# One adaLN training step on one core: w_mod's gradient blocks earlier, three kinds of stores on other queues, two transposed loads ahead of the last phase

## The chip, the cores and the metric

The kernel runs on 1 core of a Trainium2 chip. A core has a matrix engine (TensorE, PE in the profile; its weight loads are PEld), VectorE (DVE), ScalarE (ACT), GpSimd (POOL) and SyncE (SP), which here issues DMAs only. DMAs can be issued from SP's, ACT's and POOL's queues. Each engine and each queue works through its instructions in a fixed order; an instruction that waits holds up everything behind it.

The metric is device time in microseconds (us) of one execution. Before the change the median of 8 runs is 433.16 us (431.62 to 435.19).

## The reference, cut to what matters

A block of an adaptive-LayerNorm network, its output and the gradients of nine of its inputs. S = 2048 rows, D = 512 columns, F = 1792 hidden columns, all in bf16.

```
mod = silu(c) @ w_mod                        # six rows of D: sa, ca, ga, sb, cb, gb
h = layernorm(x) * (1 + ca) + sa
x = x + ga * irfft2(rfft2(h) * (w_r + 1j * w_i))
h = layernorm(x) * (1 + cb) + sb
x = x + gb * (relu(h @ w1 + b1) ** 2 @ w2 + b2)
# jax.vjp of this with grad_out:
# returns x and the gradients of x, w_r, w_i, w1, b1, w2, b2, c, w_mod
```

The kernel's outputs are numbered 0 (x), 1 (gradient of x), 2 and 3 (w_r, w_i), 4 (w1), 5 (b1), 6 (w2), 7 (b2), 8 (c) and 9 (w_mod, 512 x 3072, computed in six column blocks of 512).

## The kernel before, in words

Rows sit on the 128 partitions, 16 rows each, so that x is a tile of 128 x 16 x 512 and a "row tile" t holds 128 rows. Fourier transforms are products with small cosine and sine matrices. The kernel has four stretches in time:

1. 0 to about 93 us: layernorm, the forward spectral filter, and the product of grad_out with w2 (`back_products`, line 700).
2. 93 to 282 us: the dense part in four blocks of 512 rows (`stage_h`, `stage_o`, `stage_gn`). It leaves in DRAM what the end needs: `h_dram` (the hidden activations), `n1_dram` (normalised rows) and `gx1_dram` (a part of x's gradient).
3. 282 to about 352 us, the way back through the filter (lines 1049 to 1204). `spec_f23` (line 299) runs over eight groups gi. For each, PE makes psB and psC, ACT copies them (AE, then G, line 313), and DVE does the complex products of `ew_b` (line 1140, `cmul` line 414): first Z times G, which `spec_g1` will need, then X times G, the gradient gW of the filter, which goes out in four stores per group (line 1146; six for group 0). After each group `after_b` (line 1148) loads a later group and calls `fill_w1`, which puts one or two of 16 units of w1's gradient on PE (`grad_w1`, line 1100: 16 products of 128 x 448, one copy by ACT at line 1108, and after each second unit one store at line 1110). After groups 1, 3, 5 and 7 it calls `GMod.emit` (line 452), a block of w_mod's gradient, here "gm block". Then `spec_g1` (line 336) multiplies the eight Z by LG; its 16 results are copied out of PSUM by DVE (line 351) and ACT (line 353) in turn, four PSUM buffers at a time.
4. 352 us to the end. Eight row pairs (`row_pair`, line 1240, t = 0, 2, ... 14) finish x's gradient; each is a chain of ACT copies of psY (line 1249), DVE work (lines 250 to 270 and 1251 to 1265), two ACT sums (line 1253) and a store of gx (line 1266). A row pair reads `n1` at line 1254 and `gxl` at line 1265; `load_rows3` (line 1190) loads them two row pairs ahead into two buffers each, so a load has to wait until the row pair before last has read its buffer. Between row pairs 14 units of w2's gradient run (`grad_w2`, line 1170): 16 products of 128 x 512 with `hn` and `g_sb`, a DVE product into gw (line 1176, three buffers), a store (line 1177). `hn` is a transposing load from `h_dram` (line 1168), 512 KB each; `g_sb` is grad_out, 2 MB, one load at line 1196. Two more gm blocks and c's gradient end the kernel.

A gm block broadcasts one gradient row over the partitions with PE (line 457), copies it with ACT (gmbc, one buffer, line 459), scales it by silu(c) into gwm (two halves by ACT, two by DVE, lines 467 and 469) and stores gwm (line 472); and it multiplies four 128 x 512 pieces of w_mod (wmc, loaded at line 463) with gmbc on DVE and sums them (gm_junk, line 470).

The order of the work is set when the program is built: the code is written in a rough order with priorities, a list scheduler orders each engine and queue, and semaphores are put in. Tiles come from pools with a number of buffers (`bufs`). Pools are stacked from the left and from the right end of the on-chip memory, so a new pool may lie where an old one was, and its first user then waits for the old one's last readers, stores among them. PSUM for the units (`mm`) has two buffers.

Nearly all DMAs of stretches 3 and 4 are issued by SP, stores included. POOL issues only the loads of w_r and w_i in stretch 1 (line 548), ACT three small loads at the start.

Of the kernel before, what the change touches and what calls it, by code (L numbers as in the profile page):

```python
# [12 lines left out]
BF16 = mybir.dt.bfloat16  # L13
# [430 lines left out]
class GMod:  # L444
# [3 lines left out]
    def __init__(self, tc, K, scf, gsc, wm_view, out9_view):  # L448
        self.__dict__.update(locals())
        self.bufs = 2  # L450

    def emit(self, jc, q, row, pool, ppool):

        nc, K = self.tc.nc, self.K
        cs = slice(jc * D, (jc + 1) * D)
        psb = ppool.tile([P, D], FP32, name="mm")
        nc.tensor.matmul(psb, lhsT=K["ones_sq"][q:q + 1, :], rhs=row, start=True, stop=True, tile_position=(q, 0))
        gmbc = pool.tile([P, D], BF16, name="gmbc", bufs=1)
        nc.scalar.copy(out=gmbc, in_=psb)
        junk = pool.tile([P, D], BF16, name="gm_junk", bufs=1)  # L460
        for dc in range(0, 4, 2):
            wmc = pool.tile([P, 2, D], BF16, name="wmc", bufs=self.bufs)
            nc.sync.dma_start(wmc, self.wm_view[:, dc:dc + 2, cs])
            gwm = pool.tile([P, 2, D], BF16, name="gwm", bufs=self.bufs)
            for i in range(2):
                if i == 0:
                    nc.scalar.activation(gwm[:, i, :], gmbc, AF.Copy, scale=self.scf[:, dc + i:dc + i + 1])
                else:
                    nc.vector.tensor_scalar(gwm[:, i, :], gmbc, self.scf[:, dc + i:dc + i + 1], None, op0=ALU.mult)
                nc.vector.scalar_tensor_tensor(out=junk, in0=wmc[:, i, :], scalar=K["onef"], in1=gmbc, op0=ALU.mult, op1=ALU.mult,  # L470
                                               accum_out=self.gsc[:, jc, dc + i:dc + i + 1])
            nc.sync.dma_start(self.out9_view[:, dc:dc + 2, cs], gwm)


@with_exitstack
def kernel(
# [571 lines left out]

    gm = GMod(tc, K, scf, gsc, wm_view, out9_view)
    lf2 = tc.alloc_tile_pool(name="lf2", bufs=1, side="right")  # L1050
    K["LF"] += [lf2.tile([P, 2, 3, P], BF16, name=f"LFb{gi}") for gi in range(4, 8)]
    W4 = 448
# [47 lines left out]
    def grad_w1(fb, dc):  # L1100
        fs = slice(fb * W4, (fb + 1) * W4)
        ps = mmps.tile([P, SB], FP32, name="mm")
        for t in range(NT):
            nc.tensor.matmul(ps[:, 0:W4], lhsT=h2_sb[:, t, dc * P:(dc + 1) * P], rhs=ghn[t // 4][:, t % 4, fs],  # L1104
                             start=(t == 0), stop=(t == NT - 1))
        if fb % 2 == 0:
            w1o[0] = gwa.tile([P, 2, W4], BF16, name="gw1", bufs=2)
        nc.scalar.copy(out=w1o[0][:, fb % 2, :], in_=ps[:, 0:W4])  # L1108
        if fb % 2 == 1:
            nc.sync.dma_start(out4_view[:, dc, (fb - 1) * W4:(fb + 1) * W4], w1o[0].rearrange("p a f -> p (a f)"))  # L1110

# [7 lines left out]
    def fill_w1(n):  # L1119
        for _ in range(n):  # L1120
            if units:
                units.pop(0)()

    gms = [lambda j=j, q=q, row=row: gm.emit(j, q, row, gwa, mmps)
           for j, q, row in ((5, 0, grow[0:1, :]), (2, 32, grow[32:33, :]), (3, 64, grow[64:65, :]), (4, 0, gcrow))]

    with tc.tile_pool(name="f23b", bufs=2) as fr, tc.tile_pool(name="ewb", bufs=2) as ew:
# [9 lines left out]
        for gi in range(4):  # L1137
            load(gi)

        def ew_b(gi, G):  # L1140
# [3 lines left out]
            for i, o in enumerate((out_2, out_3)):  # L1144
                for p0_, n, rows_ in w_parts(o, gi):
                    nc.sync.dma_start(rows_, gW[p0_:p0_ + n, i, :, 0:DF])

        def after_b(gi):
# [4 lines left out]
            fill_w1(2 if 0 < gi < 6 else 1)  # L1153
            if gi % 2 == 1:
                gms.pop(0)()

        spec_f23(tc, K, UT, AEs, None, lambda gi: gwa.tile([P, 2, 2, FP], BF16, name="G", bufs=2), ew_b, after_b)
    lf2.release()
    gwp = tc.alloc_tile_pool(name="gwp", bufs=1, side="right")
    g_sb = gwp.tile([P, NT, D], BF16, name="g_sb")  # L1160

    hns, endp = [], {}

    def load_hn():
        fc = len(hns)
        if fc < NFC:
            hns.append(endp.get("hn", gwp).tile([P, NT, P], BF16, name="hn", bufs=4))
            nc.sync.dma_start(hns[fc], h_dram[fc, :, :], transpose=True)

    def grad_w2(fc):  # L1170
# [4 lines left out]
        with tc.high_priority():  # L1175
            nc.vector.tensor_tensor(gw, ps, modb[:, GB_B, :], op=ALU.mult)  # L1176
        nc.sync.dma_start(out6_view[:, fc, :], gw)
        load_hn()
# [16 lines left out]

    nc.sync.dma_start(g_sb, g_view)
    load_hn()
    load_rows3(0)
    load_rows3(2)
    for _ in range(3):  # L1200
        load_hn()
# [9 lines left out]
    def fill(n):  # L1211
        for _ in range(n):
            if units:
                fill_w1(1)
                if not units:
                    gwa.release()
                    gap.release()
                    gm.bufs = 4
                    endp["hn"] = endp["gm"] = tc.alloc_tile_pool(name="endp", bufs=2)
# [8 lines left out]
    with tc.tile_pool(name="psE", bufs=2, space=PSUM) as psE, tc.tile_pool(name="psS1", bufs=1, space=PSUM) as psS1:  # L1228
# [11 lines left out]
        def row_pair(t, Ts):  # L1240
# [65 lines left out]
    fin.release()  # L1306
    gwp.release()
    h2p.release()
    cdp.release()
# [36 lines left out]
```

## Time and profile before

| what | value |
|---|---|
| time of the profiled execution | 433.14 us |
| its span (first to last instruction) | 431.4 us |
| median of 8 runs | 433.16 us (431.62 to 435.19) |
| PE busy | 400.2 us, 93% |
| DVE busy | 353.6 us, 82% |
| ACT busy | 256.4 us, 59% |
| POOL busy | 41.1 us, 10%, nothing after slice 6 |
| DMA | 101.11 MB, 234 GB/s on average |
| mean granted clock of TensorE | 0.99 |

The profile gives for every engine how long it was busy, what it waited for (the releaser), and the chain of waits that ended last. A table of windows gives the busy time of each engine in a stretch. "DMA share" is the time that packets took, over 16 DMA engines; it goes above 1 where packets overlap. SPq stands for SP's queue, and the time of an SPq instruction is how long SP was held by issuing it. Idle time before an instruction is shown in square brackets with what ended it. The profile shortens names: `n` is n1, `gh` is gh1, `q` is q1, `jk` is jk1.

### The profile page before, as it was taken

What the parts mean: (1) busy time and instruction counts of PE and PEld (TensorE: products, weight loads), DVE (VectorE), ACT (ScalarE), POOL (GpSimd) and SP (SyncE); (2) the same over time, 40 slices, a digit from 0 to 9 for tenths busy, and PEclk for the clock granted to TensorE, in tenths of its full rate; (3) what the DMA queues carried; (4) which work ended last, traced back from release to release, by engine and by line L of the source; (5) the groups of instructions that cost most, each with busy time, mean ns of one, the idle gap of its engine ahead of it and who ended that gap; (6) DMA issues with size and microseconds to landing.
All of it is one profiled execution on the core that took longest, in us unless ns stands there. A gap on an engine that the chain in (4) does not pass through costs nothing.

```text
span 431.4 us, 7120 instructions
## 1 busy us (share of the span) xinstructions
PE 400.2 (93%) x2375; PEld 196.4 (46%) x2375; DVE 353.6 (82%) x864; ACT 256.4 (59%) x487; POOL 41.1 (10%) x114
## 2 busy tenths in 40 slices
PE   2789999999899999999999999999999899995996
PEld 0345446654434444444444444455565564441332
DVE  6799868959996588978897998929587968988796
ACT  5578699778882188248635855474348375445231
POOL 8347940000000000000000000000000000000000
PEclk9999999999999999999999999999999999998899
DMA  8998899979497459768965997997895599999974
GB/s 245 243 271 247 244 214 313 311 227 231 136 352 233 131 102 336 197 168 193 289 174 177 196 325 255 287 241 222 266 299 174 166 278 285 235 243 263 260 212 136
DMA packets 147147, 101.11 MB, mean 234 GB/s; under 512 B 98945, under 2 KB 131590, under 8 KB 146726
## 3 DMA queue, kind: packets, MB, share of 16 engines
q1 hardware_dynamic: 145458, 98.01, 83.8%
q0 software_dynamic: 1088, 2.11, 2.1%
q10 hardware_dynamic: 564, 0.53, 0.4%
q8 instruction: 19, 0.31, 0.3%
q14 instruction: 18, 0.15, 0.1%
HBM read 35.44 MB, written 41.60 MB: 179 GB/s over the span
## 4 chain that ended last, share of the span: by engine, by line
PE 41%; DVE 24%; ACT 16%; DMA 10%; issue 5%; SPq 2%; POOL 1%; ACTq 0%; DVEq 0%
PE og L901 12%; PE mm L872 10%; PE mm L707 5%; PE mm L1173 4%; DVE gm_junk L470 2%; DMA LGb<-LG_dram 2%; DMA xs_dram<-Xs 2%; ACT gab L712 2%; PE psG L346 2%; DMA n<-n_dram 2%; ACT AE L329 1%; DVE p L419 1%; DMA h_dram<-h 1%; ACT Xs L313 1%; DMA out_dram<-gW 1%
## 5 line engine op out<-in xcount | busy, mean ns | idle before, releaser
L707 PE MATMUL mm<-gT,w2T 128*128 128x512 bf16 x224 | 58.1, 385 | 2.9 <-ACT gab L712 2.9
L1173 PE MATMUL mm<-g_sb,hn 128*128 128x512 bf16 x224 | 53.0, 392 | 3.9 <-DVE gw L1176 3.9
L872 PE MATMUL mm<-h2T,w 128*128 128x512 bf16 x224 | 53.4, 378 | 1.3 <-ACT r L874 1.2
L901 PE MATMUL og<-w1T,gab 128*128 128x512 bf16 x224 | 50.9, 379 | 0.8 <-DVE o L966 0.7
L1104 PE MATMUL mm<-gab,h_sb 128*128 128x448 bf16 x256 | 51.2, 352 | 0.0
L901 PE MATMUL og<-w,h 128*128 128x512 bf16 x224 | 50.1, 379 | 0.0
L874 ACT ACTIVATE r<-mm,b1col 128x512 bf16<-128x512 f32 x56 | 37.0, 686 | 6.1 <-PE mm L872 3.3
L1173 PEld LDWEIGHTS <-hn 128*128 128x128 bf16 x224 | 21.6, 100 | 31.1 <-issue 8.9
L872 PEld LDWEIGHTS <-w 128*128 128x128 bf16 x224 | 21.1, 97 | 30.0 <-issue 8.3
L1104 PEld LDWEIGHTS <-h_sb 128*128 128x128 bf16 x256 | 24.6, 98 | 21.3 <-issue 0.6
L901 PEld LDWEIGHTS <-h 128*128 128x128 bf16 x224 | 21.7, 97 | 26.2 <-issue 1.0
L901 PEld LDWEIGHTS <-gab 128*128 128x128 bf16 x224 | 21.6, 98 | 25.9 <-issue 1.4
L707 PEld LDWEIGHTS <-w2T 128*128 128x128 bf16 x224 | 21.3, 99 | 22.7 <-issue 6.8
L914 ACT CAST G<-og 128x512 bf16<-128x512 f32 x16 | 9.2, 581 | 28.1 <-PE og L901 28.1
L876 DVE TENSOR_TENSOR h<-r 128x1024 bf16<-128x1024 bf16 x28 | 19.2, 685 | 4.8 <-ACT r L874 4.8
L712 ACT CAST gab<-mm 128x512 bf16<-128x512 f32 x36 | 21.4, 601 | 2.2 <-PE mm L707 2.0
L1253 ACT ACTIVATE gs<-gn,inv 128x512 bf16<-128x512 bf16 x16 | 11.4, 716 | 17.4 <-DVE gn L1251 17.4
L1108 ACT CAST gw<-mm 128x448 bf16<-128x448 f32 x16 | 8.7, 543 | 21.1 <-DMA out_dram<-gw 10.4
L710 DVE CAST gab<-mm 128x512 bf16<-128x512 f32 x20 | 13.8, 688 | 8.0 <-PE mm L707 7.8
L377 ACT ACTIVATE Tsb<-psT 128x512 bf16<-128x512 f32 x32 | 18.5, 605 | 2.0 <-PE psT L375 1.5
L470 DVE SCALAR_TENSOR_TENSOR gm_junk<-wmc,onef,gmbc 128x512 bf16<-128x512 bf16 x24 | 17.9, 745 | 2.1 <-DMA wmc<-in_w_mod_dram 1.2
L880 DVE TENSOR_TENSOR gab<-r,gab 128x1024 bf16<-128x1024 bf16 x28 | 19.1, 683 | 0.0
(289 smaller groups left out, 768.5 us busy)
## 6 DMA issues: line engine op xcount, KB each, us to landing
h_dram<-h SPq DMA_DIRECT2D x28, 256.0 KB, 3.4
gh_dram<-gab SPq DMA_DIRECT2D x28, 256.0 KB, 4.0
w<-in_B_w_dram SPq DMA_DIRECT2D x2, 1792.0 KB, 8.8
wmc<-in_w_mod_dram SPq DMA_DIRECT2D x12, 256.0 KB, 4.2
out_dram<-gwm SPq DMA_DIRECT2D x12, 256.0 KB, 2.6
wz_dram<-Z SPq DMA_DIRECT2D x8, 258.0 KB, 3.6
xs_dram<-Xs SPq DMA_DIRECT2D x8, 258.0 KB, 2.8
Z<-wz_dram SPq DMA_DIRECT2D x8, 258.0 KB, 4.5
```

The lines of the kernel that those rows point to most:

```text
L377: nc.scalar.activation(Tsb, ps, AF.Copy, scale=EF_S)
L470: nc.vector.scalar_tensor_tensor(out=junk, in0=wmc[:, i, :], scalar=K["onef"], in1=gmbc, op0=ALU.mult, op1=ALU.mult, accum_out=self.gsc[:, ...
L707: nc.tensor.matmul(ps, lhsT=w2T[:, dc, fc * P:(fc + 1) * P], rhs=gT[b][:, :, dc, :], start=(dc == 0), stop=(dc == 3))
L710: nc.vector.tensor_copy(out=gaT[b][:, fc, :], in_=ps)
L712: nc.scalar.copy(out=gaT[b][:, fc, :], in_=ps)
L872: nc.tensor.matmul(ps, lhsT=w1[:, dc, (fc + i) * P:(fc + i + 1) * P], rhs=h2T[b][:, :, dc, :], start=(dc == 0), stop=(dc == 3))
L874: nc.scalar.activation(r[:, i, :], ps, AF.Relu, bias=b1col[:, fc + i:fc + i + 1])
L876: nc.vector.tensor_tensor(h2, r, r, op=ALU.mult)
L880: K["gh"] = nc.vector.tensor_tensor(gh, r, gh, op=ALU.mult).ins
L901: nc.tensor.matmul(ps, lhsT=lhs(fc), rhs=rhs[:, fc, :], start=(fc == 0), stop=(fc == NFC - 1))
L1104: nc.tensor.matmul(ps[:, 0:W4], lhsT=h2_sb[:, t, dc * P:(dc + 1) * P], rhs=ghn[t // 4][:, t % 4, fs], start=(t == 0), stop=(t == NT - 1))
L1173: nc.tensor.matmul(ps, lhsT=hns[fc][:, t, :], rhs=g_sb[:, t, :], start=(t == 0), stop=(t == NT - 1))
```

## The change

- `GMod` no longer loads its wmc pieces inside `emit`. A new `load` does, called one gm block ahead, with four buffers. The gm blocks of stretch 3 come after groups 0, 1, 3 and 4 instead of 1, 3, 5 and 7, and have their own pool, `gmp`, on the right.
- gwm is stored from POOL's queue (it was SP's).
- w1's gradient is stored from ACT's queue, with four buffers (it was SP's, two).
- The first two `hn` loads go into a pool of their own, `hnp`, and are placed behind the gW stores of group 5 on SP. The pool `gwp` then holds two more, and `endp` four as before: eight buffers in all, as before.
- w2's gradient and x's gradient are stored from POOL's queue.

No arithmetic changes, and no bytes are added or left out.

```diff
 class GMod:
     def __init__(self, tc, K, scf, gsc, wm_view, out9_view):
-        self.bufs = 2
+        self.tiles = {}
+
+    def load(self, jc, pool):
+        cs = slice(jc * D, (jc + 1) * D)
+        self.tiles[jc] = [pool.tile([P, 2, D], BF16, name="wmc", bufs=4) for _ in range(2)]
+        for dc in range(0, 4, 2):
+            self.tc.nc.sync.dma_start(self.tiles[jc][dc // 2], self.wm_view[:, dc:dc + 2, cs])
     def emit(self, jc, q, row, pool, ppool):
...
-            wmc = pool.tile([P, 2, D], BF16, name="wmc", bufs=self.bufs)
-            nc.sync.dma_start(wmc, self.wm_view[:, dc:dc + 2, cs])
-            gwm = pool.tile([P, 2, D], BF16, name="gwm", bufs=self.bufs)
+            wmc = self.tiles[jc][dc // 2]
+            gwm = pool.tile([P, 2, D], BF16, name="gwm", bufs=2)
...
-            nc.sync.dma_start(self.out9_view[:, dc:dc + 2, cs], gwm)
+            nc.gpsimd.dma_start(self.out9_view[:, dc:dc + 2, cs], gwm)
...
+    hnp = tc.alloc_tile_pool(name="hnp", bufs=1, side="right")
+    hns, endp = [], {}
+
+    def load_hn():
+        fc = len(hns)
+        if fc < NFC:
+            pool = hnp if fc < 2 else endp.get("hn", endp["gw"])
+            hns.append(pool.tile([P, NT, P], BF16, name="hn", bufs=2 if pool is not endp.get("hn") else 4))
+            nc.sync.dma_start(hns[fc], h_dram[fc, :, :], transpose=True)
+
     lf2 = tc.alloc_tile_pool(name="lf2", bufs=1, side="right")
+    gmp = tc.alloc_tile_pool(name="gmp", bufs=1, side="right")
...
         if fb % 2 == 0:
-            w1o[0] = gwa.tile([P, 2, W4], BF16, name="gw1", bufs=2)
+            w1o[0] = gwa.tile([P, 2, W4], BF16, name="gw1", bufs=4)
...
-            nc.sync.dma_start(out4_view[:, dc, (fb - 1) * W4:(fb + 1) * W4], ...)
+            nc.scalar.dma_start(out4_view[:, dc, (fb - 1) * W4:(fb + 1) * W4], ...)
...
         for gi in range(4):
             load(gi)
+            if gi == 1:
+                gm.load(gms[0][0], gmp)
...
-                    nc.sync.dma_start(rows_, gW[p0_:p0_ + n, i, :, 0:DF])
+                    K["gW"] = nc.sync.dma_start(rows_, gW[p0_:p0_ + n, i, :, 0:DF]).ins
...
             fill_w1(2 if 0 < gi < 6 else 1)
-            if gi % 2 == 1:
-                gms.pop(0)()
+            if gi == 5:
+                with tc.issue_after(K["gW"]):
+                    load_hn()
+                    load_hn()
+            if gi in (0, 1, 3, 4):
+                gms.pop(0)[1]()
+                if gms:
+                    gm.load(gms[0][0], gmp)
...
+    gmp.release()
     lf2.release()
...
-        nc.sync.dma_start(out6_view[:, fc, :], gw)
+        nc.gpsimd.dma_start(out6_view[:, fc, :], gw)
         load_hn()
...
     nc.sync.dma_start(g_sb, g_view)
-    load_hn()
     load_rows3(0)
     load_rows3(2)
-    for _ in range(3):
+    for _ in range(2):
         load_hn()
...
-            nc.sync.dma_start(out1_view[:, t:t + 2, :], gx)
+            nc.gpsimd.dma_start(out1_view[:, t:t + 2, :], gx)
             load_rows3(t + 4)
...
         for j in range(2):
+            gm.load(j, endp["gm"])
             gm.emit(j, 32 * j, acc1_sb[32 * j:32 * j + 1, :], endp["gm"], psX)
```

The built program has the same instructions as before in the same order on every engine up to about 282 us.

More of the change, by code (lines that the diff above doesn't have):

```diff
@@ L1106, in grad_w1 @@
         if fb % 2 == 0:
-            w1o[0] = gwa.tile([P, 2, W4], BF16, name="gw1", bufs=2)
+            w1o[0] = gwa.tile([P, 2, W4], BF16, name="gw1", bufs=4)
         nc.scalar.copy(out=w1o[0][:, fb % 2, :], in_=ps[:, 0:W4])
         if fb % 2 == 1:
-            nc.sync.dma_start(out4_view[:, dc, (fb - 1) * W4:(fb + 1) * W4], w1o[0].rearrange("p a f -> p (a f)"))
+            nc.scalar.dma_start(out4_view[:, dc, (fb - 1) * W4:(fb + 1) * W4], w1o[0].rearrange("p a f -> p (a f)"))
     units = []
@@ L1122, in fill_w1 @@
                 units.pop(0)()
-    gms = [lambda j=j, q=q, row=row: gm.emit(j, q, row, gwa, mmps)
+    gms = [(j, lambda j=j, q=q, row=row: gm.emit(j, q, row, gmp, mmps))
            for j, q, row in ((5, 0, grow[0:1, :]), (2, 32, grow[32:33, :]), (3, 64, grow[64:65, :]), (4, 0, gcrow))]
@@ L1160 @@
     g_sb = gwp.tile([P, NT, D], BF16, name="g_sb")
[L1162 to L1168, printed above, removed]
+    endp["gw"] = gwp
     def grad_w2(fc):
@@ L1217, in fill @@
                     gap.release()
-                    gm.bufs = 4
                     endp["hn"] = endp["gm"] = tc.alloc_tile_pool(name="endp", bufs=2)
@@ L1307 @@
     gwp.release()
+    hnp.release()
     h2p.release()
```

## The prediction

> **What bounds the kernel now.** First the windows of the way back, 10 us each. The columns are window and length, then busy us and instruction count of PE, PEld, DVE, ACT and POOL, then granted clock, DMA share and GB/s.
>
> ```profile
> 310.00:320.00 10.00, 10.00 (x62) 5.52 (x61) 7.87 (x20) 6.20 (x12) 0.00 (x0) 1.00 0.96 300
> 330.00:340.00 10.00, 9.71 (x84) 5.88 (x83) 9.96 (x26) 7.23 (x14) 0.00 (x0) 1.00 0.60 169
> 340.00:350.00 10.00, 8.51 (x70) 6.04 (x69) 9.92 (x23) 3.75 (x7) 0.00 (x0) 1.00 0.66 197
> 360.00:370.00 10.00, 10.00 (x56) 4.58 (x54) 9.76 (x26) 4.38 (x10) 0.00 (x0) 1.00 1.14 277
> 390.00:400.00 10.00, 5.04 (x23) 1.59 (x23) 8.13 (x23) 5.06 (x12) 0.00 (x0) 0.78 1.07 245
> ```
>
> Until 330 PE is full, and what ACT or DVE lose there costs nothing. From 330 DVE is full, and PE stays close behind. From 350 the DMA engines are full too. Three resources near their limit leave little: PE is idle 1.5 us in 340 to 350 and 5.0 us in 390 to 400, where its clock falls to 0.78 as well. Only there, and at the start of the last phase, can time be won. Next the waits after 350, then after 280 (us in total, times, longest):
>
> ```profile
> DVE q L1254 <- DMA n<-n_dram: 4.1, 3, 1.9
> PE mm L1173 <- DVE gw L1176: 3.9, 1, 3.9
> DVE gw L1176 <- PE mm L1173: 2.4, 2, 2.2
> ...
> ACT gw L1108 <- DMA out_dram<-gw: 10.4, 2, 5.5
> ```
>
> DVE waits for a load of n1, PE then for DVE's gw behind it, and DVE later for the delayed PE. Why n1 is late stands in the timeline of SP (start, us, what):
>
> ```profile
> 345.81 0.35 SPq L1196 DMA_DIRECT2D g_sb<-in_grad_out_dram  x1
> 346.21 7.16 SPq L1168 DMA_TRANSPOSE hn<-h_dram  x1
> 353.42 0.57 SPq L1193 DMA_DIRECT2D n<-n_dram  x1
> ...
> 376.93 5.61 SPq L1168 DMA_TRANSPOSE hn<-h_dram  x2
> 382.64 0.53 SPq L1193 DMA_DIRECT2D n<-n_dram  x1
> ...
> 386.94 4.32 SPq L1168 DMA_TRANSPOSE hn<-h_dram  x1
> 391.37 0.52 SPq L1193 DMA_DIRECT2D n<-n_dram  x1
> ```
>
> Each late n1 stands behind a transposing load that holds SP for 2 to 7 us. Last, DVE at the end of the filter:
>
> ```profile
> 340.88 0.42 DVE L421 TENSOR_TENSOR gW<-p 128x514 bf16<-128x514 bf16 x1
> 341.22 0.74 DVE L470 SCALAR_TENSOR_TENSOR gm_junk<-wmc,onef,gmbc 128x512 bf16<-128x512 bf16 x1
> ...
> 343.76 0.68 DVE L351 CAST utcs<-psG 128x512 bf16<-128x512 f32 x1
> ```
>
> The first copy of spec_g1 stands behind the fourth gm block.
>
> **The change part by part.** The sum is against the profiled execution, 433.14 us (span 431.4 and 1.74 around it), which is the median of the runs, 433.16, within 0.02.
>
> *Gm blocks earlier.* On DVE one costs four gm_junk with their reads (0.743 + 0.080 us) and two gwm (0.345): 4.0 us. In 280 to 330 DVE idles 8.1 us for the first Z, 8.1 for G and 1.2 for wmc. These 17 us take the two moved blocks (8 us), because wmc is loaded one block ahead. The third block no longer stands in front of group 6: its G is there at 332.7, work began at 333.66, so 1 us earlier. Group 7 ends at 340.3 instead of 341.3, the first copy starts there instead of at 343.76, and the last phase's first psT comes 3.5 to 4.5 us earlier than 352.0. On ACT gmbc now waits for the gm block before (one buffer) and AE stands behind it: some 2 us near 298, covered by a full PE. If that cover fails, its psC is late by the same 2 us.
>
> *Two hn in front, and what stands behind them.* In the new SP stream hn0 and hn1 come before the eight gW stores of groups 6 and 7, then g_sb, and n1 of the first row pair directly behind g_sb. Group 5's stores ended at 332.6. Two issues at 2.0 to 2.5 us (the shortest rows; the DMA share there is only 0.60) end near 337, the eight stores follow group 7 by 342.4, and g_sb, which waited for the last store's landing, starts near 345.0 (345.81 before). From 345.81 until DVE had n1 at 358.02, g_sb, hn0 and n1 landed: 2.75 MB in 12.2 us, 225 GB/s. Without hn0 it is 2.25 MB, 10.0 us: n1 at 355.0, so 3.0 us earlier. This ends later than the gm gain, so the start of the row pairs moves by 3.0 us and not by the sum. Ends: 4.8 (at the 309 GB/s of 346 to 354) and 0 (see the first rival).
>
> *Stores off SP.* From 363.9 to 399.4 SP issues 13 stores at about 0.45 us, 5.9 us, with their waits in the same queue. The n1 of row pair 8 was issued at 382.64 though its buffer had been read at 376.2; that of row pair 10 at 391.37, its buffer read at 384.6. In the new stream no transposing load stands between n1 of pair 6 and n1 of pair 10: wmc four times, gxl, n1, gxl, n1. DVE lost 1.16 and 1.87 us on these two loads, and 2.17 us at 403 because PE had stood 3.9 us and then run slow (12 products in 4.3 us, later 12 in 2.7). All of it is 5.2 us. But n1 of pair 6 now has three hn directly in front (7.6 us for three at 356.26, some 10 us at the 3.2 us median), where it had one. I count the later load with its consequence, 4.0, less 0.8 for pair 6: 3.2. Ends: 5.2 and 0.
>
> *w1's stores on ACT.* Eight issues at about 0.51 us (SP's rows for them). ACT's two waits of 10.4 us on these stores go; PE was full beside them, worth 0. Six issues lie beside full PE, two between the psY copies of the first row pairs, where n1 is later anyway: 0.4 lost, ends 0 and 1.0.
>
> *Stores on POOL.* POOL did nothing after 280, so 34 issues are free room. In the one stretch with POOL DMAs (38 to 60 us) an issue took 0.54 to 0.81 us and landed after 2.7 to 5.6. A gw store on SP landed after 1.7 to 5.7. gw has three buffers, at least 10 us, and gx two, some 14: no wait. The last gw store is on the path: 0.3 us more to issue and 0.5 more to land, 0.8 lost, ends 0 and 3.0. DVE beside POOL's issues:
>
> ```profile
> L548 POOL DMA_DIRECT2D Z<-in_A_w_r_dram x17: 553/607/813, 38.2 to 57.9; - x17
> ...
> L622 DVE TENSOR_SCALAR gT<-gT,gb2x x16: 340/345/442, 14.9 to 77.1; 128x512 bf16<-128x512 bf16 x16
> ```
>
> At most 0.1 us on one of 20 such instructions (gn, gwm) in the last phase: 0.3 lost, ends 0 and 2.
>
> Sum: 3.0 + 3.2 - 0.4 - 0.8 - 0.3 = 4.7 us earlier, 428.4 us.
>
> Two rules speak against this. The Trainium skill, "SBUF — State Buffer", Summary: rules for kernel authors, says that a GpSimd-queue DMA should not be hidden under DVE work, since its descriptors starve while DVE is in a fast mode, and gives some 3.1 us instead of 0.62 for one DMA. The rows above show POOL issues of 0.6 us beside such DVE work. By the page the last store would cost 2.5 us more and the sum would be about 430.9. The other, "DMA: Bandwidth & Descriptors", Rules for kernel authors: spreading DMAs over queues brings no bandwidth, it saves issue time only; by that alone the n1 stalls would stay and the sum would be 431.6, which is the second rival.
>
> **The rivals.**
>
> *Slower: the two hn hold up g_sb.* One mechanism: SP, between group 5's and group 6's stores. With an issue time x each, the stores end near 332.6 + 2x + 5, and g_sb starts 2.5 us later. At x = 4.1 g_sb starts at 348, n1 lands at 358 as before, and the start gains nothing; beyond it all is later by 2x - 8.2. At the longest row, 7.16, that is 6 us: with the stalls saved (3.2) and the losses (1.5) 433.14 + 6.0 - 1.7 = 437.4. For it: two of 14 rows are over 4.1 (7.16, 4.32). Against it: the 7.16 stood behind 2 MB, and the share at 330 to 350 is 0.60 to 0.66.
>
> *The queues were not the limit.* The DMA share is 1.0 to 1.23 from 354 to 410. Then a load issued earlier lands no earlier, the stalls stay, and only the 1 MB in front counts: 433.14 - 3.0 + 1.5 = 431.6. For it: the share. Against: n1 landed in 3.2 to 4.6 us once issued, and was issued over 6 us after its buffer was free.
>
> *Everything fits.* DVE after 358.02 has 63.1 us of work in the 70.2 us until its last gw. Start 4.8 earlier, all 5.2 saved, no loss: 423.1. PE allows it: 224 products at 0.2205, 34 at 0.194 and some 12 us of small ones from 347.5 end at 415.5, the last gw before at 427.56. Against: the same DMA bytes in less time.
>
> *The stores on POOL hurt more.* All their upper ends, 3.0 and 2, instead of 0.8 and 0.3: 432.3.
>
> **How the numbers follow.** Forecast 0.45 (its own range 425.5 to 431), queues not the limit 0.18, everything fits 0.15, slower 0.15, POOL 0.07. About 0.5% (2.2 us) is what a measurement of this kernel tells from no change: faster is below 431.0, slower above 435.3. Faster: the forecast but for 0.02, all of "fits", 0.07 of 0.18 and 0.02 of POOL: 0.67. Slower: 0.12 of the first rival and 0.01 elsewhere: 0.13. The rest, 0.20, is the same. Below 423.5 lies half of "fits", above 434.5 most of the first rival: the range 423.5 to 434.5 leaves out two in ten.
>
> **What would show it.** Right: the first DVE copy at L351's place right after the last gW and before 342; hn0 and hn1 near 333 for 2 to 3 us each; g_sb at or before 346; DVE's wait for n1 below 2 us in total; no dip of the clock near 395; POOL issues below 1 us. Wrong: hn0 and hn1 over 4 us each, or gW stores behind them; a new wait of n1 at row pair 6; PE waiting for gw as before; POOL issues of several us, or DVE's gn above 0.45 us; ACT held at gmbc for longer than PE's work covers. The forecast is wrong if the DMA engines, not SP, decide when n1 lands, or if a moved transposing load holds the stores behind it.

## The result and the profile after

The changed kernel takes 439.08 us (median of 11 runs, 437.41 to 441.7), the kernel before, beside it, 433.17 (32 runs): a ratio of 1.0141, 95% interval 1.0114 to 1.0167. It is slower by some 6 us, 10.7 above the forecast of 428.4 and above the upper end of its range, 434.5. The profiled execution took 438.43 us with a span of 436.6, 5.2 more than the 431.4 of before.

The windows of the way back after the change, columns as before:

```profile
310.00:320.00 10.00, 7.28 (x46) 3.95 (x45) 9.46 (x24) 5.54 (x12) 0.11 (x1) 1.00 0.77 235
330.00:340.00 10.00, 10.00 (x66) 6.00 (x65) 9.17 (x21) 6.95 (x13) 0.73 (x1) 1.00 0.49 145
340.00:350.00 10.00, 8.52 (x97) 6.31 (x95) 8.88 (x17) 4.64 (x8) 0.00 (x0) 1.00 0.73 152
360.00:370.00 10.00, 10.00 (x64) 4.97 (x62) 7.54 (x17) 4.99 (x13) 0.58 (x1) 1.00 1.16 278
390.00:400.00 10.00, 6.81 (x42) 2.68 (x35) 9.62 (x23) 6.15 (x15) 2.20 (x5) 0.92 1.13 269
```

PE has a hole of 2.7 us in 310 to 320, where it was full before. The old hole in 390 to 400 is smaller (6.81 busy instead of 5.04, clock 0.92 instead of 0.78). The waits, the first two from the list after 350, the others from the list of 280 to 350 (us in total, times, longest):

```profile
DVE q L1271 <- DMA n<-n_dram: 2.8, 2, 2.4
...
PE mm L1192 <- DVE gw L1195: 2.2, 1, 2.2
...
ACT gw L1124 <- DMA out_dram<-gW: 9.0, 2, 4.5
...
DVE gm_junk L475 <- DMA wmc<-in_w_mod_dram: 5.0, 2, 3.8
...
ACT gwm L472 <- DMA out_dram<-gwm: 3.8, 2, 2.1
...
DVE gwm L474 <- DMA out_dram<-gwm: 3.0, 2, 1.6
...
PE mm L1120 <- ACT gw L1124: 2.7, 1, 2.7
```

DVE's waits for n1 shrank from 4.1 to 2.8 us. ACT's 10.4 us for w1's buffers went, but 9.0 us for something else came in the same place: the landing of gW stores, which are SP's. New, too, are the waits of ACT and DVE for gwm stores to land, and DVE's waits for wmc grew from 1.2 to 5.0 us. The rows of ACT and of its queue near 310, those of w1's units alone, show where the 9.0 us are spent:

```profile
304.58 0.56 ACT L1124 CAST gw<-mm 128x448 bf16<-128x448 f32 x1
309.25 0.36 ACTq L1126 DMA_DIRECT2D out_dram<-gw  x1
309.65 0.53 ACT L1124 CAST gw<-mm 128x448 bf16<-128x448 f32 x1 [4.50 <-DMA out_dram<-gW]
...
312.20 0.60 ACT L1124 CAST gw<-mm 128x448 bf16<-128x448 f32 x1
316.86 0.35 ACTq L1126 DMA_DIRECT2D out_dram<-gw  x1
317.25 0.53 ACT L1124 CAST gw<-mm 128x448 bf16<-128x448 f32 x1 [4.46 <-DMA out_dram<-gW]
```

The copy was done at 305.1, but ACT issued its store at 309.25 only, and its next copy after that: ACT stood in front of its own store. In the built program the DMAs of SP and ACT in this stretch share eight completion semaphores, taken in turn, and each DMA first waits for the one that used its semaphore before. The eight w1 stores are scattered among SP's DMAs, so such a store may go only when a DMA of SP has landed. SP's rows behind the filter:

```profile
327.09 11.56 SPq L1164 DMA_DIRECT2D out_dram<-gW  x8
338.70 5.35 SPq L1063 DMA_TRANSPOSE hn<-h_dram  x2
344.16 5.11 SPq L1164 DMA_DIRECT2D out_dram<-gW  x8
352.45 0.36 SPq L1215 DMA_DIRECT2D g_sb<-in_grad_out_dram  x1
352.86 0.42 SPq L1212 DMA_DIRECT2D n<-n_dram  x1
```

g_sb starts 6.6 us later than before (352.45 instead of 345.81). The chain of work that ended last runs over the last gW store and two loads of n1 (start, us, what):

```profile
348.66 3.40 DMA out_dram<-gW
...
352.86 9.23 DMA n<-n_dram
...
380.64 3.38 DMA n<-n_dram
```

DVE's rows at the end of the filter, the first use of n1 and the last gw:

```profile
343.61 0.42 DVE L421 TENSOR_TENSOR gW<-p 128x514 bf16<-128x514 bf16 x1
343.94 1.28 DVE L351 CAST utcs<-psG 128x512 bf16<-128x512 f32 x2
...
362.12 0.69 DVE L1271 TENSOR_TENSOR q<-gh,n 128x1024 bf16<-128x1024 bf16 x1 [2.44 <-DMA n<-n_dram]
...
428.68 0.68 DVE L1195 TENSOR_TENSOR gw<-mm,modb 128x512 bf16<-128x512 f32 x1
```

The same two rows of before:

```profile
358.02 0.69 DVE L1254 TENSOR_TENSOR q<-gh,n 128x1024 bf16<-128x1024 bf16 x1 [1.09 <-DMA n<-n_dram]
...
427.56 0.69 DVE L1176 TENSOR_TENSOR gw<-mm,modb 128x512 bf16<-128x512 f32 x1
```

The first copy to utcs does follow the last gW directly, but at 343.94, no earlier than before (343.76). The first q comes at 362.12 instead of 358.02. From there to the last gw it is 66.6 us instead of 69.5. And from the last gw to the end of the span it is 7.9 us instead of 3.8 (436.6 - 428.68; 431.4 - 427.56). These three differences, +4.1, -3.0 and +4.1, are the 5.2 us between these two executions.

Where the last one comes from stands in the list of GpSimd's drains, the instruction by which its queue is emptied at the end of the program (shortest, median and longest in ns, first and last start). Before, then after:

```profile
L1341 POOLq DRAIN  x3: 46/98/2997, 253.9 to 431.1; - x3
```

```profile
L1360 POOLq DRAIN  x3: 46/97/6228, 429.6 to 436.4; - x3
```

Before, GpSimd had nothing to do after 254 and its drain of 3.0 us lay there, hidden. After, it starts with the last gw store and lasts 6.2 us, to 435.9. Everything else had ended by then; the store itself landed 2.2 us after its issue, so the drain does not wait for that landing.

### The profile page after: what moved, and what is told of

It reads as the page before. It is cut to its first block, busy times and chain, and to the rows that moved or that the text cites. A ratio compares the mean times of both kernels' runs of the same rounds, so it can differ in the third digit from the quotient of the medians.

```text
span 436.6 us, 7137 instructions
## 1 busy us (share of the span) xinstructions
PE 399.1 (91%) x2375; PEld 195.7 (45%) x2375; DVE 355.5 (81%) x864; ACT 256.7 (59%) x487; POOL 61.8 (14%) x148
## 4 chain that ended last, share of the span: by engine, by line
PE 36%; DVE 19%; DMA 16%; ACT 16%; SPq 6%; issue 5%; POOL 1%; ACTq 0%; POOLq 0%; DVEq 0%
PE og L906 10%; PE mm L877 7%; DMA out_dram<-gW 6%; PE mm L712 5%; PE mm L1192 4%; SPq L865 3%; DMA n<-n_dram 3%; PE psG L346 2%; ACT gab L717 2%; DMA Xb<-xs_dram 2%; DVE jk L1275 1%; ACT Xs L313 1%; ACT n2rows L940 1%; ACT AE L329 1%; ACT v L934 1%
## 5 line engine op out<-in xcount | busy, mean ns | idle before, releaser
L1192 PE MATMUL mm<-g_sb,hn 128*128 128x512 bf16 x224 | 51.7, 385 | 2.2 <-DVE gw L1195 2.2
L477 POOL DMA_DIRECT2D out_dram<-gwm x12 | 8.7, 728 | 75.3 <-DMA Z<-wz_dram 37.2
```

Source lines behind the costliest of these rows:

```text
L1192: nc.tensor.matmul(ps, lhsT=hns[fc][:, t, :], rhs=g_sb[:, t, :], start=(t == 0), stop=(t == NT - 1))
```

## The experiments

The chips differ: the kernel before took 433.2 to 436.3 us. So times are told as ratios to the kernel before on the same chip; 1% is 4.3 us. The difference of two ratios carries the root of the summed squares of their half intervals. All kernels compute everything. "Tail" is the time from the start of the last gw to the end of the span.

A trace is one execution. In the six traces of kernels that equal the one before up to the last phase (itself and five variants below that move only stores of that phase), the first copy to utcs lies at 343.8 to 346.5, g_sb at 345.8 to 349.5 and the first q at 358.0 to 362.2, and the trace of before is the earliest in all three. So a difference of a few us between two traces shows where time goes, not how much. The tail is steadier: 3.8 to 3.9 us in the eleven traces, granted clock near 0.99, whose stores near the end are all SP's.

### First: each suspected loss undone or made alone

Only the last gw store from GpSimd, on the kernel before:

```diff
-        nc.sync.dma_start(out6_view[:, fc, :], gw)
+        (nc.gpsimd if fc == NFC - 1 else nc.sync).dma_start(out6_view[:, fc, :], gw)
```

> The kernel before, with one DMA moved: the store of the last gradient of w2 (gw of fc 13) is issued by GpSimd instead of SP. Theory (GpSimd's queue takes long to be drained after its last DMA, and here that drain ends the program: 6.2 us in the trace after, against 3.84 us from the last gw to the end before): the end moves back by 2.2 to 4.2 us, to 435.5 to 437.5, with a drain of GpSimd of 5 to 6.5 us as the last thing in the trace. Rival (only the landing of one store from GpSimd is a little later, as the prediction had it): +0.5 to +1, 434.

Measured: 1.0009 (0.998 to 1.0039). The tail is 5.66 us instead of 3.84, and it ends with a drain:

```profile
L1341 POOLq DRAIN  x3: 46/98/3563, 430.0 to 434.1; - x3
```

So here the drain ends the program, but it is 3.6 us long and not 6. The tail grew by 1.8, less than the theory's 2.2, and the time doesn't show it: its interval ends at +1.7 us.

The stores near the end back on SP, on the changed kernel:

```diff
-        nc.gpsimd.dma_start(out6_view[:, fc, :], gw)
+        (nc.gpsimd if fc < 10 else nc.sync).dma_start(out6_view[:, fc, :], gw)
...
-            nc.gpsimd.dma_start(out1_view[:, t:t + 2, :], gx)
+            (nc.gpsimd if t < 14 else nc.sync).dma_start(out1_view[:, t:t + 2, :], gx)
...
-            nc.gpsimd.dma_start(self.out9_view[:, dc:dc + 2, cs], gwm)
+            (nc.gpsimd if jc > 1 else nc.sync).dma_start(self.out9_view[:, dc:dc + 2, cs], gwm)
```

> The changed kernel, with the stores near the end back on SP (gw from fc 10, gx of the last pair, the gwm of the last two blocks); GpSimd's last DMA then lies some 25 us ahead of the end. Theory (GpSimd's drain ends the program): the 4.1 us between after's and before's tail come back, about 435.0 from 439.1. Rival (GpSimd has to be drained at the end whenever it has issued DMAs in the last phase, or the tail is long because of the other stores on SP): 438 to 439.

Measured: 1.005 (1.0022 to 1.0078), which is 0.91 ± 0.39% below the changed kernel, 3.9 us. The tail is 3.88, and the long drain lies beside the work, from 418.4:

```profile
L1360 POOLq DRAIN  x3: 46/98/6223, 418.4 to 435.6; - x3
```

The theory holds: 4.1 us in the traces, 3.9 in the times.

w1's stores back on SP, on the changed kernel:

```diff
-            nc.scalar.dma_start(out4_view[...], ...)
+            nc.sync.dma_start(out4_view[...], ...)
```

> The changed kernel, with the stores of w1's gradient back on SP, still with four buffers. Theory (a store issued by ACT waits for DMAs of SP, 9.0 us in the trace after, and PE loses 2.7 us at 317.8 for it): PE's hole at 317.8 goes, psC of the last group and the first copy to utcs come 2.5 to 3.5 us earlier, and the time falls by 2 to 3, to about 436.5. Rival (the stores of gwm from GpSimd land 8 to 9 us after their issue and hold the way back in the same place): no change, 438.5 to 439.5.

Measured: 1.0132 (1.0096 to 1.0168), no better than the changed kernel. ACT's wait for gW and PE's hole are gone, psC of the last group starts 1.2 us earlier (334.86; no more than traces differ), but g_sb starts at 352.44 as before the edit. The rival is right on the time; what holds g_sb this run does not tell.

The hn loads behind g_sb, on the changed kernel:

```diff
-            if gi == 5:
-                with tc.issue_after(K["gW"]):
-                    load_hn()
-                    load_hn()
...
     nc.sync.dma_start(g_sb, g_view)
+    load_hn()
     load_rows3(0)
     load_rows3(2)
-    for _ in range(2):
+    for _ in range(3):
         load_hn()
```

> The changed kernel, with hn0 and hn1 no longer ahead of the gW stores of groups 6 and 7: the first hn stands behind g_sb and three behind the rows, as in the kernel before. Theory (the two hn take 5.35 us of SP's queue and hold up g_sb by 6.6 us against before): g_sb starts near 346 to 347, q1 of pair 0 ends 2.5 to 4 us earlier, and the time falls to 435.5 to 436.5. Rival (the bytes are the limit, and each order of them ends at the same time): n1 of a later pair waits longer by what the first gains, 439.

Measured: 1.0145 (1.01 to 1.019). It did not do what was meant: since the pool `hnp` was free, the scheduler moved the two loads ahead, to 285 and 323.67, where the second held SP for 7.6 us and the sixteen last gW stores behind it. It tells only that these places are no better.

### Second: several undone together, and the parts that are left

All three undone. The hn loads come from `gwp` as in the kernel before, `hnp` is gone, and the two edits above for the end and for w1's stores are in:

```diff
-            pool = hnp if fc < 2 else endp.get("hn", endp["gw"])
-            hns.append(pool.tile([P, NT, P], BF16, name="hn", bufs=2 if pool is not endp.get("hn") else 4))
+            hns.append(endp.get("hn", endp["gw"]).tile([P, NT, P], BF16, name="hn", bufs=4))
```

> The changed kernel with three things undone: the stores near the end on SP, w1's stores on SP (four buffers stay), and the hn loads all behind g_sb from the pool they had before (the variant with the hn late had moved two of them to 285 and 324 us, since their pool was free then; here they can't). What is left of the change: the four gm blocks earlier with their loads ahead, and GpSimd's queue for the gwm, gw and gx stores up to some 25 us before the end. Theory (the tail cost 4.1 and the two hn ahead of the gW stores 2 to 3): the time falls below that of the kernel before by 1 to 3 us (0.2 to 0.7 per cent). Rival (the bytes that lie between 285 and 370 us are the limit, and their order is worth nothing): like the run with the end alone on SP, 0.5 per cent above before.

Measured: 0.9956 (0.9923 to 0.9989): below the kernel before by 1.9 us, and 0.94 ± 0.43% below the one with the end alone on SP. So the two hn and w1's stores together cost 4.1 ± 1.9 us. In its trace g_sb starts at 346.24 and the first copy to utcs at 341.10.

The same with w1's stores on ACT (`nc.scalar` again at `out4_view`):

> As the one above, but w1's stores stay on ACT. Theory (w1's stores on ACT cost nothing by themselves: the run with them back on SP lost ACT's wait for gW and the time stayed): within 0.3 per cent of the one above. Rival (ACT's waits behind SP's DMAs cost 2 to 3 us once the other losses are gone): 0.5 to 0.7 per cent above it.

Measured: 1.0032 (0.9999 to 1.0065), 0.76 ± 0.47% above the one before. The rival: here w1's stores on ACT cost 3.3 ± 2.0 us. PE's windows show the hole and, behind it, a lower clock:

```profile
310.00:320.00 10.00, 5.85 (x39) 3.17 (x38) 8.88 (x21) 4.36 (x9) 0.00 (x0) 1.00 0.70 191
320.00:330.00 10.00, 10.00 (x54) 5.05 (x53) 8.26 (x22) 5.79 (x11) 1.45 (x2) 0.83 0.99 360
```

The gm blocks alone: from the run with all three undone, every `nc.gpsimd` store of gwm, gw and gx back to `nc.sync`.

> The kernel before with the gm blocks alone changed: earlier in the filter stage, with wmc loaded ahead, every store on SP, the hn behind g_sb, four w1 buffers. Theory (without the late landing of the gwm stores from GpSimd and without the two hn the first copy to utcs comes 3 us earlier, and 2 to 3 of it reach the end): 0.5 to 0.7 per cent below before. Rival (n1 of the later pairs comes when the DMA engines have moved what lies ahead, and takes back what was won): within 0.3 per cent of before.

Measured: 0.9952 (0.9923 to 0.9982). The theory holds for the time, though the interval reaches into the rival's 0.3%. GpSimd's queue is not needed for it: with it the ratio was 0.9956.

On the kernel before, gw (fc 0 to 9) and gx (all but the last) from GpSimd:

```diff
-        nc.sync.dma_start(out6_view[:, fc, :], gw)
+        (nc.gpsimd if fc < 10 else nc.sync).dma_start(out6_view[:, fc, :], gw)
...
-            nc.sync.dma_start(out1_view[:, t:t + 2, :], gx)
+            (nc.gpsimd if t < 14 else nc.sync).dma_start(out1_view[:, t:t + 2, :], gx)
```

> The kernel before with one part alone: the gw stores of fc 0 to 9 and the gx stores but the last from GpSimd, all other stores on SP. Theory (n1 waits on SP's queue behind stores; 5.2 us of DVE's waiting for n1 are in the trace before): part of it goes, 2 to 3 us, 0.5 to 0.7 per cent below before. Rival (n1 waits for the DMA engines, not for the queue): within 0.3 per cent of before.

Measured: 1.001 (0.9978 to 1.0043). The theory fell. DVE still waits for n1, as long as before (4.1):

```profile
DVE q L1254 <- DMA n<-n_dram: 4.5, 1, 4.5
```

### Third: the two hn alone, and other queues

The end and w1's stores on SP, the two hn ahead of the gW stores as in the change:

> The changed kernel with the stores near the end and w1's stores back on SP; the two hn stay ahead of the gW stores of groups 6 and 7. Against the run with all three undone (0.44 per cent below before) it differs by the two hn alone. Theory (the two hn delay the gW stores and g_sb by 5 to 6 us and n1 by as much): 2 to 3.5 us above that run, 0.1 to 0.4 per cent above before. Rival (the two hn are 10 us of DMA that the last phase then need not do, and repay what they hold up): within 0.3 per cent of the run with all three undone.

Measured: 1.0021 (0.9993 to 1.0048), 0.65 ± 0.43% above the run with all three undone, 2.8 us. The theory holds. SP's rows, to be set beside those of the run with all three undone, which come second:

```profile
333.70 3.27 SPq L1164 DMA_DIRECT2D out_dram<-gW  x4
337.02 4.82 SPq L1063 DMA_TRANSPOSE hn<-h_dram  x2
...
342.58 5.15 SPq L1164 DMA_DIRECT2D out_dram<-gW  x8
351.85 0.36 SPq L1215 DMA_DIRECT2D g_sb<-in_grad_out_dram  x1
```

```profile
333.33 3.26 SPq L1162 DMA_DIRECT2D out_dram<-gW  x4
...
337.32 6.06 SPq L1162 DMA_DIRECT2D out_dram<-gW  x8
346.24 0.35 SPq L1209 DMA_DIRECT2D g_sb<-in_grad_out_dram  x1
```

Group 5's stores (first row of each) end near 336.8 in both, 4.2 us later than the 332.6 of the kernel before. The two hn then take 4.8 us, and g_sb starts 5.6 us later. Over all traces with the gm blocks earlier, from the end of group 5's stores to g_sb it takes 13.8 to 15.4 us in the six with the two hn between, 9.6 to 12.6 in the six where every hn follows g_sb.

w1's stores from GpSimd, on the run with all three undone (`nc.gpsimd` at `out4_view`):

> The run with all three undone, but w1's stores from GpSimd's queue instead of SP's. Theory (what costs 3 us when ACT issues these stores is that ACT stands behind its own store until DMAs of SP have landed, and with it the copies that PE waits for; GpSimd has nothing behind a store that PE waits for): no hole of PE between 305 and 325, and within 0.3 per cent of the run with all three undone. Rival (the bytes of these stores, leaving early beside the gW stores, hold up Z, Xb and wmc whatever the queue): the hole stays, 0.5 to 0.8 per cent above that run.

Measured: 1.0002 (0.9964 to 1.0039), 0.46 ± 0.50% above the run with all three undone. PE is full from 300 to 330 (8.3 us of the next 10), so the hole there is ACT's doing, as the theory has it. The time stands between the two and settles nothing.

Only the last gw store back on SP, on the changed kernel:

```diff
-        nc.gpsimd.dma_start(out6_view[:, fc, :], gw)
+        (nc.gpsimd if fc < NFC - 1 else nc.sync).dma_start(out6_view[:, fc, :], gw)
```

> The changed kernel with the last store of gw alone moved from GpSimd to SP; GpSimd's last DMA is then the last gwm, some 2 us earlier. Theory (the drain of GpSimd lasts some 6 us from its last DMA, whatever that is): the tail from the start of the last gw to the end falls from 7.9 to about 6, and the time by 2 (0.4 per cent). Rival (the landing of the last store is what ends the program): tail about 4, and the time falls by 4 (0.9 per cent).

Measured: 1.0155 (1.0107 to 1.0203), not faster than the changed kernel; the gain of 0.4% that was expected lies within the uncertainty of 0.55%. The tail is 6.16 us, as the theory said. The drain starts with the last gwm store (433.70) and lasts as long as in the changed kernel:

```profile
L1360 POOLq DRAIN  x3: 46/98/6308, 433.7 to 440.5; - x3
```

The rows ahead of the first hn, on the run with all three undone: `load_rows3(0)` and `load_rows3(2)` moved in front of the first `load_hn()`.

> The run with all three undone, with the rows (n1 and gxl of pairs 0 and 1) ahead of the first hn on SP. Theory (n1 of pair 0 was issued at 353.7, behind 7 us of the first hn, and q of pair 0 waited some 1.5 us for it): q of pair 0 comes 1 to 1.5 us earlier, n1 of the later pairs as before; 0 to 0.3 per cent below that run. Rival (w2's first products wait for the hn and PE stands instead): 0.2 to 0.5 per cent above it.

Measured: 0.9981 (0.9936 to 1.0026), 0.25 ± 0.56% above that run: nothing that can be told. In its trace the first q is not earlier (358.42, there 357.81).

### Fourth: one thing added to the gm blocks

The gm blocks alone, once more:

> The kernel with the gm blocks alone changed, once more, beside the two below that add one thing to it, so that each is compared on the same chip, and for a trace of it at full clock. Theory: 0.3 to 0.7 per cent below before; in the trace the first copy to utcs some 2.5 us earlier, at 341 to 342, and g_sb where before has it. Rival (the gain needs GpSimd's queue for the gwm stores): within 0.3 per cent of before.

Measured: 0.9964 (0.9934 to 0.9995). With the first reading the mean is 0.42 ± 0.21% below before, 1.8 us. In its trace, 0.7 us shorter than that of before, the gain is not where the theory had it: the first copy to utcs is 1.5 us earlier (342.30), but n1 was issued at 354.94 and the first q is 1.1 later than before (359.11). The gain comes in the last phase, where DVE's wait for n1 is 0.9 us instead of 4.1 and PE's hole in 390 to 400 is smaller. The wait and the window:

```profile
DVE q L1266 <- DMA n<-n_dram: 0.9, 1, 0.9
```

```profile
390.00:400.00 10.00, 7.05 (x34) 3.02 (x33) 9.74 (x25) 6.07 (x14) 0.00 (x0) 0.85 1.12 273
```

With w1's stores on ACT (`nc.scalar` at `out4_view`):

> The kernel with the gm blocks alone changed, and w1's stores on ACT: nothing of the change is on GpSimd, and the hn are where before has them. Theory (ACT stands behind its own stores until DMAs of SP have landed, and PE behind ACT): a hole of PE of 2.5 us or more between 300 and 325, and 0.5 to 0.8 per cent above the run with the gm blocks alone. Rival (the loss needs GpSimd's late gwm stores): within 0.3 per cent of it.

Measured: 0.9957 (0.9916 to 0.9997), the same as without. There is a hole of PE of 2.24 us that ends at 324.6 and ACT's wait of 5.4 us for gW, yet no loss that shows (-0.3 ± 2.2 us): the rival.

With the two hn ahead of the gW stores, every store on SP:

> The kernel with the gm blocks alone changed, and the two hn ahead of the gW stores of groups 6 and 7, every store on SP. Theory (g_sb and n1 stand behind the two hn and the gW stores that follow): g_sb 5 us or more later than in the run with the gm blocks alone, and 0.4 to 0.8 per cent above it. Rival (what the two hn hold up is repaid in the last phase): within 0.3 per cent of it.

Measured: 1.002 (0.9982 to 1.0058), 0.56 ± 0.49% above the gm blocks alone, 2.4 us. g_sb starts at 355.82 instead of 347.42; 3.5 us of that lie ahead of the hn, where group 5's stores end at 341.25 instead of 337.70. The theory holds, a second time: the mean of the two readings is 0.61 ± 0.33%, 2.6 us.

The last gw from GpSimd as two DMAs, on the kernel before:

```diff
-        nc.sync.dma_start(out6_view[:, fc, :], gw)
+        if fc < NFC - 1:
+            nc.sync.dma_start(out6_view[:, fc, :], gw)
+        else:
+            for i in range(2):
+                nc.gpsimd.dma_start(out6_view[:, fc, i * 256:(i + 1) * 256], gw[:, i * 256:(i + 1) * 256])
```

> The kernel before, with the store of the last gw issued by GpSimd as two DMAs of half the columns each. One such store gave a drain of 3.56 us; where two or more DMAs had been issued shortly before, it lasted 6.2 to 7.3. Theory (the drain takes about 3 us for each DMA that is still under way): a drain of 6 us or more, and a tail of 7.5 to 8.5 us from the start of the last gw. Rival (the drain goes by the bytes or by the landing): 3.5 to 4, a tail of 5.7 to 6.3.

Measured, one execution: 435.53 us. The tail is 6.28, 0.6 more than with one DMA, which is about the second issue. The drain is not counted in DMAs:

```profile
L1345 POOLq DRAIN  x3: 46/98/3698, 429.3 to 433.5; - x3
```

### Fifth: what makes the drain long

The last four gw from GpSimd (`fc >= 10`), on the kernel before:

> The kernel before, with the stores of the last four gw (fc 10 to 13, some 4 us apart) from GpSimd. One such store, in one DMA or in two, gave a drain of 3.6 to 3.7 us; where GpSimd had also stored gwm or gx, 6.2 to 7.3. Theory (what GpSimd has stored over the last phase counts, not the last DMA alone): a drain of 5 us or more, a tail of 7 or more from the start of the last gw. Rival (only what is under way counts, or the kind of store): 3.5 to 4, a tail of 5.7 to 6.3.

Measured, one execution: 440.69 us beside 436.31 for the kernel before. A drain of 3.74 us and a tail of 5.48: three stores before it do not make it long. The rest of the 4.4 us lies ahead of the last gw, which came at 433.42; one pair of runs doesn't tell it from chance.

The last gwm alone from GpSimd (`jc == 1 and dc == 2`), on the kernel before:

> The kernel before, with the very last gwm store alone (256 KB, one DMA, some 2 us ahead of the last gw) from GpSimd. Theory (a store of twice the bytes, 256 packets of 1 KB in place of 128, is what makes the drain long): a drain of 6 us or more from about 426, so an end some 2 to 3 us later than before's. Rival (the size does not matter): a drain of 3.5 to 4, which ends before the landing of the last gw from SP, and a tail of 3.8 to 4.2 as in the kernel before.

Measured, one execution: 437.39 us beside 436.31. A drain of 4.10 us from 430.6 and a tail of 3.85: it just hides. Twice the bytes add half a microsecond in this trace, no more. What separates 3.6 to 4.1 us from the 6.2 and more that were found wherever GpSimd had made 17 to 34 stores in the last 150 us stays open.

### The sum

From the kernel before to the changed one, each step by the pair of kernels that differ in it alone:

| step | ratios | us |
|---|---|---|
| gm blocks earlier | mean of 0.9952 and 0.9964 | -1.8 ± 0.9 |
| gwm, gw and gx from GpSimd, but not near the end | 0.9956 against that mean | -0.1 ± 1.7 |
| two hn ahead of the gW stores | 1.0021 against 0.9956 | +2.8 ± 1.9 |
| w1's stores on ACT, on top of that | 1.0050 against 1.0021 | +1.3 ± 1.7 |
| the stores near the end from GpSimd | 1.0141 against 1.0050 | +3.9 ± 1.7 |

They must add up to the whole 6.1 us, since each ends where the next begins. The fourth step comes out differently in other surroundings: +3.3 ± 2.0 without the two hn, +0.4 ± 1.9 in the changed kernel, -0.3 ± 2.2 with the gm blocks alone. Only the gm blocks, the two hn and the stores near the end are clear of zero.

## Why the prediction was wrong, point by point

*Gm blocks earlier.* "Group 7 ends at 340.3" and the first copy there: it was 341.10 with all three undone and 342.30 with the gm blocks alone, 343.94 in the whole change. That the first copy follows the last gW is right. What failed is "These 17 us take the two moved blocks (8 us), because wmc is loaded one block ahead": in the changed kernel DVE waits 5.0 us for wmc and 3.0 for gwm stores inside these blocks, where before it waited 1.2 and nothing, so from 285 to 340 it is busy 40.1 us, hardly more than before (39.2), though all four blocks lie there and not three. A load one block ahead in the program still stood behind six gW stores on SP: it was issued at 302.62, and DVE waited 3.8 us for it, until 307.19. The gain of 3 us at the start of the row pairs is not there (first q 1.1 us later with the gm blocks alone, 0.2 earlier with all three undone). The working saw that the third block no longer stands in front of group 6; it did not see that the fourth now stands in front of group 5. Group 5's last gW ended at 330.4 before, at 333.6 with all three undone and at 336.5 in the changed kernel. ACT's wait at gmbc was 2.2 us beside a full PE, as said.

*Two hn in front.* Here the start of the row pairs was lost. "Group 5's stores ended at 332.6" was taken over from the order of before; after, they ended at 338.65 (332.6 to 335.3 in the six traces like before, 336.2 to 341.7 in the thirteen with the gm blocks earlier). Of the 7.5 us by which g_sb missed 345.0 that is 6.0. The two hn took 5.35 us instead of 4.4, near the estimate of 2.0 to 2.5 each and far from the 4.1 at which the rival was to begin, and the last landing took 3.2 instead of 2.6. So g_sb was held up, as in *Slower: the two hn hold up g_sb*, but not for that rival's reason: the place itself had moved back. The first q came 4.1 us later, not 3.0 earlier; by the times, the two hn cost 2.6 us where they were to help win 3.0. (The upper end of 4.8 goes by a g_sb at 345.81; from the 345.0 of the same sum, 2.25 MB at 309 GB/s would make it 5.7.)

What moved group 5 on from 333.6 to 336.5 is in part in the changed kernel's rows: DVE stood 3.0 us in the fourth gm block for gwm stores from GpSimd, issued at 319.89 and 320.82 and landed 7.9 and 9.5 us later. With all three undone it stood 1.7 us in that block, for a gwm store and for wmc, so 1.4 of the 2.9 us come from there; 0.9 had gone before the block and 0.5 went on a wait for G behind it. "gw has three buffers ... no wait" left gwm out, which has two.

*Stores off SP.* The size is right by luck, the reason is not. From the first q to the last gw 3.0 us were saved, where 3.2 were counted. But the stores alone on GpSimd saved nothing (1.001) and DVE's wait for n1 stayed, while the gm blocks alone took it from 4.1 to 0.9 with every store still on SP. From the first q to the last gw it takes 68.4 to 71.2 us in the six traces like before, and 65.9 to 67.8 in the three with the gm blocks earlier and gwm, gw and gx all on SP; why the earlier gm blocks do this stays open. The n1 of row pair 6 was issued at 380.64 behind three hn (9.45 us), as feared, and cost DVE 0.3 us. PE still waited for gw, 2.2 us instead of 3.9, and the clock near 395 was 0.92: two of the signs for this step came true by half. A rule of the Trainium skill, "DMA: Bandwidth & Descriptors", Rules for kernel authors, which the prediction weighed, says that spreading DMAs over queues only saves issue time; the run with the stores alone on GpSimd agrees with it.

*w1's stores on ACT.* Costed by the issue, 0.4 us. The issue took 0.34 to 0.38; what was missed is the wait in front of it. ACT stood 4.1 us twice before its own stores, and PE 2.7 us behind it. How much of that reaches the end comes out between nothing and 3.3 us by the runs, each reading with some 2 us of uncertainty, and what decides it is not settled.

*Stores on POOL.* The last gw store was costed at 0.8 us by its issue and landing, with an upper end of 3.0. Both were right as far as they went (issue 0.57, landing 2.2 us after the issue), but the drain behind it is 6.2 us long, and 4.1 us of the tail are new. The term of 0.8 measured 3.9 by the times; it is the largest single loss. On the issues and on DVE's speed the working was right:

```profile
L1196 POOL DMA_DIRECT2D out_dram<-gw x14: 540/542/570, 370.6 to 429.7; - x14
...
L1279 DVE TENSOR_SCALAR gn<-n,rr x16: 403/405/412, 364.6 to 417.9; 128x512 bf16<-128x512 bf16 x16
```

The issues stayed at 0.54 us beside a DVE that was 96% busy in 390 to 400, and gn at 0.405 us. The landings did not stay: "no wait" went by SP's landings, but the eight gwm stores of the way back took longer from GpSimd. With the gm blocks alone, from SP, and then in the changed kernel (issues in ns; to landing in us, shortest, median and longest):

```profile
L477 SPq DMA_DIRECT2D out_dram<-gwm x8: 388/410/468, 300.0 to 329.7; - x8
...
DMA to landing us min/median/max: 3.7/3.9/4.1
```

```profile
L477 POOL DMA_DIRECT2D out_dram<-gwm x8: 727/727/751, 291.0 to 331.3; - x8
...
DMA to landing us min/median/max: 3.4/6.5/9.5
```

The rule of the page "SBUF — State Buffer" (Summary: rules for kernel authors) spoke against the change: a DMA from GpSimd's queue is starved of its descriptors beside fast DVE work. The page's figure, 3.1 us instead of 0.62 (section "A bandwidth-pool intuition that's wrong (but worth ruling out)"), is for the DMA and not for its issue. The issues show nothing of it; landings that are 2.6 us longer in the median would fit it. Whether DVE's work makes them so no run tells.

*The numbers.* The forecast held that SP's queue was what mattered and that leaving it costs no more than an issue and a landing. One of the two losses that decided was named as a sign of being wrong ("gW stores behind them"), with a rival of 437.4 that came nearest, in part by luck: it put the 6.0 us down to hn issues of 7.16 us each, and had no drain. The other, an engine that still has its queue to empty after the last instruction, was not. Had the drain been on the list, the end of 3.0 us for the last store would have been 4 and more.

## What to carry to other kernels

Before a DMA is hung behind another instruction, work out anew when that instruction comes in the changed order: moving one block in front of it moved the place of the two hn by some 4.6 us (group 5's stores, mean of thirteen traces against six). A store moved to another engine's queue brings along that engine's waits on shared semaphores and its drain at the end, so the last DMA of a queue that is slow to empty should lie well ahead of the last work. The gm blocks alone, with every store on SP, are the simplest of the versions that were faster than both kernels (0.9952 and 0.9964 of the kernel before).

## What the runs showed of the hardware that was not expected

- GpSimd's drain takes time with nothing to wait for: 3.0 us in the kernel before, whose last DMA from GpSimd was issued near 59 us; 3.6 to 4.1 us after one to four DMAs; 6.2 to 7.7 us in the kernels with 17 and more stores from it in the last phases. SP's longest drain in the changed kernel took 13 ns, ACT's 0.75 us.
- A store from ACT's queue waited, in ACT's instruction stream, for the landing of DMAs of SP that it has no data in common with, only a semaphore: 9.0 us in two waits.
- gwm stores of 256 KB from GpSimd landed after 6.5 us in the median in the way back (up to 9.5), those from SP after 3.9 (up to 4.1); the issue on GpSimd took 0.73 us all the same.
